# Three conversions of weights moved, and one copy: a fused attention, mixing and gating kernel on one core

## The chip, the cores and the metric

The kernel runs on one core of a Trainium2 chip. A core has five engines that run their own instruction streams: TensorE (PE) for matrix products, VectorE (DVE), ScalarE (ACT) and GpSimd (POOL) for element-wise work, and SyncE (SP), which here issues the DMAs. They wait for one another through semaphores. The metric is the time of one execution on the device, in microseconds; the lower the better.

## The reference, cut to what matters

Three blocks follow one another. `B=4`, `S=576`, 8 heads of 64 columns, so 512 model columns.

```
scores = q @ k.T / 8, masked to a window of 32 (heads 0-3) or a dilated one of 128, step 4 (heads 4-7)
x  = softmax(scores) @ v                                  # (4, 576, 512) over all heads
theta = x @ w_theta                                       # 512 x 512
y  = w_tok_r @ (x * cos(theta)) + w_tok_i @ (x * sin(theta))   # mixes the 576 tokens
u  = x + y ;  x2 = u + relu(u @ w_ch)
h  = relu(x2 @ w_in) ;  hu, hv = halves of h's 1024 columns
v_s = w_spatial @ layernorm(hv) + b_spatial               # mixes the 576 tokens
out = (hu * v_s) @ w_out
```

Everything is float32. The kernel writes a float32 factor as a rounded high part and the remainder, and makes a float32 product of three products: high by high, high by low, low by high.

## The kernel before, in words

The inputs lie with 128 rows on the partitions. In the first phase a batch goes through four steps, named after their generators. `attention(b)` makes scores (`s`), exponentials and their sums (`sm`, L343 to L350), transposed probabilities (`pt`) and values. `th_run(b)` works on tiles `t` of 128 tokens (64 in the last). It splits x into `xh` and `xl` on DVE (L435, L436; on ACT for batch 0), multiplies by `w_theta` (`ps_th`, L441), takes the sine and cosine on ACT (`ta`, `tb`, L455 to L459), multiplies by x on DVE (L462) and splits each product into `zh` and `zl`, the cosine's in tiles 0 to 3 and the sine's in 4 to 7. `tm_run(b)` mixes the tokens (`ps_y`, L512, L519) and adds to x on DVE (L522), and that sum is split again (`uh`, `ul`). `ch_run(b)` is the channel product (`ps_r`, L540) with its eviction on DVE (L543); for batch 0 its result goes to DRAM in two parts as well, `x2p`, through two buffers named `parts`. In the second phase, `hv` and its normalisation, `hu`, the spatial product `ps_sp` and the output product `ps_o` are made batch by batch.

A weight arrives as 64-bit words in two pieces, is put together by a scaling on ACT and a shift and an or on DVE (L140 to L142), rounded to a high part, and the remainder is a subtraction on POOL. `w_in` is converted once and kept in DRAM: the value half by eight units (`j_in`, to `win_d`), the u half by two times eight (`gate_half(0)`, `gate_half(1)`, to `wiu_d`): four reads and four additions or subtractions of pieces, of which seven are written. Such a write goes through a buffer with room for both parts (`kept`), and the buffer is free when its DMA has landed. The results of `j_in` and `gate_half(0)` use the two buffers `parts`; those of `gate_half(1)` use three in the attention's pool.

What is put between what is written out by hand. `spread(main, (fill, rate))` takes one step of `main` and then `rate` steps of each fill, `late` lets a load run ahead of its conversion, and `behind` keeps a unit from being moved ahead of an instruction. Within these limits a scheduler that plans with its own costs sets the order on each engine; every engine then runs its stream in that order. The stages are

```
for b in (0, 1):
    ch = ch_run(b)
    spread(chain(tm_run(b, K_ALL), take(ch, CH_BEFORE)), (attention(b + 1), ATT_RATE), (second if b else jobs(j_tok1 + j_ch), SECOND_RATE if b else TOK_RATE))
    run(th_run(b + 1, (4, 0, 1, 2, 3) if b + 1 < PAIR else (0, 1, 2, 3)))
    run(ch)
```

then `tm_run(2)` with `attention(3)`, `third`, the theta product of the last 64 tokens of batches 2 and 3 together, `th_run(3)`, `ch_run(2)` and `tm_run(3)`.

Here `second` is `j_in + gate_half(0)` at a rate of 1.5, and `third` is `gate_half(1)`. The halves of `w_spatial` and `b_spatial` (sums and differences, high and low parts: `wsp_hh`, `wsp_lb`) are computed by `w_half` (L725) in the stage of `ch_run(3)`, together with the loads of `w_in`'s u half and the normalisation of `hv`.

Of the kernel before, what the change touches and what calls it, by code (L numbers as in the profile page):

```python
# [11 lines left out]
F32 = mybir.dt.float32  # L12
# [47 lines left out]
THETA_ENG = "gg"  # L60
Z_HI = ("v", "g")

# [5 lines left out]
def tile_block(ctx: ExitStack, tc: tile.TileContext, qT, kT, vw, eye_in, mask_in, eye_b_in, w_theta, w_tok, w_ch, w_in, w_sp, w_sph, b_sp, w_out, out):  # L68
# [21 lines left out]
    x2d = [dram.tile([P, 4, S], F32, name=f"x2d{b}") for b in range(B)]  # L90
    wo_d = dram.tile([P, 4, 2, DM], F32R, name="wo_d")
    x2p = dram.tile([P, 4, 2, S], F32R, name="x2p")
    win_d = dram.tile([P, 4, 2, DM], F32R, name="win_d")
# [72 lines left out]
    def piece(src):  # L166

        st = stg.tile([P, 2 * CH], U32, tag="w64", name="w64", bufs=4)
        SY.dma_start(st[:, :DM], src.bitcast(U32))
        return st  # L170

    def kept(src, dst, t, eng="a"):

        copy(t[:, 0], src, eng)
        G.tensor_tensor(t[:, 1], src, f32(t[:, 0]), op=ALU.subtract)  # L175
        SY.dma_start(f32(dst), f32(t))

    def stored(src, dst):

        def finish(st):  # L180
            t = p1.tile([P, 2, CH], F32R, tag="parts", name="parts", bufs=2)[:, :, :DM // 2]
            kept(bits64(None, DM // 2, IN_ENG[2], st), dst, t, IN_ENG[0])

        return lambda: piece(src), finish

    def gate_half(kk):

        g = {}
        n = DM // 2
        room = []  # L190

        def out(blk, src):
            if kk == 0:
                room.append(p1.tile([P, 2, CH], F32R, tag="parts", name="parts", bufs=2)[:, :, :n])
            elif not room:
                room.append(patt.tile([P, S + WIN], F32R, tag="k", name="wiuk", bufs=2)[:, :2 * n].rearrange("p (i n) -> p i n", i=2))
                two = patt.tile([P, NT, P], F32R, tag="v", name="wiuv", bufs=2).rearrange("p t k -> p (t k)")[:, :4 * n].rearrange("p (j i n) -> p j i n", j=2, i=2)
                room.extend((two[:, 0], two[:, 1]))
            kept(src, wiu_d[:, :, blk, kk], room.pop())

# [7 lines left out]
        def add(blk, x, y, z, op):  # L208
            def finish(_):
# [210 lines left out]
    def th_unit(b, t, pair=False):  # L420
# [39 lines left out]
        if t < 4:  # L460
            for k, tt in ((t, tb), (4 + t, ta)):
                iv = V.tensor_tensor(tt, xn, tt, op=ALU.mult)  # L462
                zh[b, k], zl[b, k] = ztile(k)
                zlast[b] = ia, iv, split(zh[b, k], zl[b, k], tt, "ag"[k // 4], "g")
        else:
# [136 lines left out]

    second = late(j_in + gate_half(0), LAG_W, last_softmax)
    third = late(gate_half(1), LAG_W, last_softmax)

# [21 lines left out]
    for b in range(PAIR):  # L627
        ch = ch_run(b)
        spread(chain(tm_run(b, K_ALL), take(ch, CH_BEFORE)), (attention(b + 1), ATT_RATE), (second if b else jobs(j_tok1 + j_ch), SECOND_RATE if b else TOK_RATE))
        run(th_run(b + 1, (4, 0, 1, 2, 3) if b + 1 < PAIR else (0, 1, 2, 3)))  # L630
        run(ch)

# [5 lines left out]
    for i in range(HELD):  # L638
        with tc.issue_after(values[12 * (PAIR + 2) - HELD + i].ins):
            next(tm)  # L640
    run(third)
    run(th_shared(PAIR))
# [81 lines left out]

    def w_half():  # L725
        st, bt = stage(), stage()
        sd, bd = (stg.tile([P, CH], F32, tag="stage", name="stage", bufs=4) for _ in range(2))
        SY.dma_start(st, w_sph)
        for r in (64, 96):
            SY.dma_start(bt[r:r + 1], b_sp)  # L730
        yield
        V.tensor_tensor(sd, st[:, :CH], st[:, CH:], op=ALU.subtract)
        for r in (64, 96):
            V.tensor_tensor(bd[r:r + 1], bt[r:r + 1, :CH], bt[r:r + 1, CH:], op=ALU.subtract)  # L734
        G.memset(f32(wsp_lb[HALF:]), 0.0)
        for s_, b_, c in ((st, bt, slice(0, 2)), (sd, bd, slice(2, 3))):
            w = CH * (c.stop - c.start)
            hh, lb = (t[:, c].rearrange("p c n -> p (c n)") for t in (wsp_hh, wsp_lb))
            A.copy(hh, s_)
            V.tensor_tensor(lb[:HALF], s_[:HALF], f32(hh[:HALF]), op=ALU.subtract)  # L740
            A.copy(lb[64:65], b_[64:65])
            bh = stage()[:, :w]
            A.copy(bh[96:97].bitcast(F32R), b_[96:97])
            V.tensor_tensor(lb[96:97], b_[96:97], bh[96:97], op=ALU.subtract)  # L744
        yield

    def w_gate(kk):
# [48 lines left out]
    wsp_hh = p2s.tile([P, 3, CH], F32R, name="wsp_hh")  # L796
    wsp_lb = p2s.tile([P, 3, CH], F32R, name="wsp_lb")
    wo_h = p2s.tile([P, 4, DM], F32R, name="wo_h")
    wo_l = p2s.tile([P, 4, DM], F32R, name="wo_l")
# [51 lines left out]

    spread(ch_run(3), (chain(jobs([lambda: win_u_load(slice(0, 4)), lambda: win_u_load(slice(4, 7))]), w_half()), 0.5), (jobs([lambda t=t: hv_norm(0, t) for t in (0, 2, 1, 3)]), HV_RATE))
    wo_load()
# [303 lines left out]
```

## Time and profile before

| what | value |
|---|---|
| median of 3 runs (lowest, highest) | 536.91 us (536.36, 539.77) |
| the profiled execution, its own time | 539.95 us |
| its span | 538.2 us |
| PE, DVE, ACT, POOL busy | 96%, 66%, 56%, 40% |
| mean granted clock of PE | 0.987 of full speed |

The profiled execution lasted 1.75 us longer than its span, which is what lies around the first and last instruction. In a timeline row the first number is the start from the span's beginning, the second the time from that start to the end of the instruction or of the few that are grouped (`x3`); matmuls are pipelined and overlap. What stands in brackets at the end is how long the engine had been idle before it, and whose end is taken to have released it. A line number is one of the kernel before.

### The profile page before, as it was taken

To read this page: it belongs to the slowest core of one execution; us is meant where nothing else is said; L and a number is where in the kernel's file an instruction comes from. 1 tells how busy PE (TensorE), PEld (TensorE's weight loads), DVE (VectorE), ACT (ScalarE), POOL (GpSimd) and SP (SyncE) were. 2 spreads that over 40 slices of the span, in tenths; PEclk is the share of its full clock that TensorE was granted. 3 is DMA by queue.
4 is the path that set the end of the run, shared out by engine and by line. 5 is a ranking of instruction groups with operands and counts; after the bars stand their busy time and mean duration, and the time that the engine had idled before them with its cause. 6 is when DMAs were issued, how large, how long until landed. Compare 5 with 4: busy or idle time off the path is not lost. (4 is left out here: it accounts for less than half of the span.)

```text
span 538.2 us, 10595 instructions
## 1 busy us (share of the span) xinstructions
PE 514.8 (96%) x3764; PEld 471.2 (88%) x3764; DVE 354.7 (66%) x888; ACT 301.3 (56%) x838; POOL 215.3 (40%) x272
## 2 busy tenths in 40 slices
PE   5979989999999989999999999989999999999997
PEld 5856879988999969999889999889899789988996
DVE  2777779546656765657563588698982929799350
ACT  4878976537866537766472253355454435555332
POOL 3874875533864427515186235202401400040040
PEclk9979989999999999999999999989999999999999
DMA  8949266750557962325005949542022030201003
GB/s 229 312 166 281 73 177 201 237 177 12 159 139 217 275 219 81 100 80 181 22 1 191 367 144 363 185 159 88 2 79 88 1 117 2 89 1 60 21 1 99
DMA packets 63193, 72.55 MB, mean 135 GB/s; under 512 B 25410, under 2 KB 46402, under 8 KB 62884
## 3 DMA queue, kind: packets, MB, share of 16 engines
q1 hardware_dynamic: 60916, 71.32, 42.0%
q10 hardware_dynamic: 2224, 0.55, 0.5%
q8 instruction: 30, 0.49, 0.4%
q14 instruction: 23, 0.19, 0.1%
HBM read 52.20 MB, written 19.66 MB: 134 GB/s over the span
## 5 line engine op out<-in xcount | busy, mean ns | idle before, releaser
L413 POOL TENSOR_TENSOR gl<-hu,gh 128x288 fp32r<-128x288 f32 (+1 forms) x32 | 30.8, 975 | 144.4 <-ACT gh L117 121.8
L519 PE MATMUL ps_y<-wtok_h,zh 128*128 128x288 f32 x270 | 82.1, 306 | 1.6 <-DVE sm L343 1.6
L519 PE MATMUL ps_y<-wtok_h,zl 128*128 128x288 f32 x270 | 80.7, 300 | 0.0
L519 PE MATMUL ps_y<-wtok_l,zh 128*128 128x288 f32 x270 | 80.3, 298 | 0.0
L519 PEld LDWEIGHTS ps_y<-wtok_h,zh 128*128 128x128 f32 x270 | 51.2, 190 | 2.7 <-DVE sm L343 1.9
L519 PEld LDWEIGHTS ps_y<-wtok_h,zl 128*128 128x128 f32 x270 | 51.3, 191 | 0.3
L519 PEld LDWEIGHTS ps_y<-wtok_l,zh 128*128 128x128 f32 x270 | 51.2, 190 | 0.1
L350 POOL TENSOR_TENSOR sm<-sm,l 128x288 f32<-128x288 f32 x48 | 32.0, 669 | 40.5 <-DVE l L349 25.6
L347 ACT ACTIVATE sm<-sm,m 128x96 f32<-128x96 f32 x108 | 39.2, 365 | 6.3 <-DVE m L344 6.0
L540 PE MATMUL ps_r<-uh,wch_h 128*128 128x288 f32 x128 | 38.0, 297 | 0.3 <-DVE x L543 0.3
L540 PE MATMUL ps_r<-ul,wch_h 128*128 128x288 f32 x128 | 37.4, 296 | 0.0
L540 PE MATMUL ps_r<-uh,wch_l 128*128 128x288 f32 x128 | 37.4, 294 | 0.0
L413 POOL TENSOR_TENSOR ul<-x,uh 128x288 fp32r<-128x288 f32 x32 | 26.6, 838 | 24.7 <-ACT uh L117 24.5
L331 PE MATMUL s<-kt,qz 128*128 128x96 f32 x252 | 36.3, 284 | 0.0
L175 POOL TENSOR_TENSOR parts<-w64g,parts 128x256 fp32r<-128x256 f32 x23 | 18.0, 784 | 43.2 <-DVE parts L119 27.6
L331 PEld LDWEIGHTS s<-kt,qz 128*128 128x128 f32 x252 | 34.0, 203 | 0.7
L923 PE MATMUL ps_sp<-wsp_h,vh 128*128 128x288 f32 x112 | 32.6, 297 | 0.3 <-ACT vh L117 0.3
L923 PE MATMUL ps_sp<-wsp_h,vl 128*128 128x288 f32 x112 | 32.9, 295 | 0.0
L441 PE MATMUL ps_th<-wth_h,xl 128*128 128x512 f32 (+1 forms) x76 | 30.2, 397 | 2.6 <-DVE xl L436 2.6
L923 PE MATMUL ps_sp<-wsp_l,vh 128*128 128x288 f32 x112 | 32.6, 294 | 0.0
L441 PE MATMUL ps_th<-wth_h,xh 128*128 128x512 f32 (+1 forms) x76 | 31.0, 410 | 0.7 <-DVE xh L435 0.7
L441 PE MATMUL ps_th<-wth_l,xh 128*128 128x512 f32 (+1 forms) x76 | 29.8, 392 | 0.0
(232 smaller groups left out, 1598.8 us busy)
## 6 DMA issues: line engine op xcount, KB each, us to landing
vt<-vw SPq DMA_DIRECT2D x15, 576.0 KB, 5.5
w<-w_tok SPq DMA_DIRECT2D x18, 288.0 KB, 4.5
x2d<-x SPq DMA_DIRECT2D x32, 144.0 KB, 2.8
kt<-kT SPq DMA_DIRECT2D x15, 304.0 KB, 4.2
w<-w_in SPq DMA_DIRECT2D x16, 256.0 KB, 3.8
out<-o SPq DMA_DIRECT2D x15, 256.0 KB, 2.0
qz<-qT SPq DMA_DIRECT2D x26, 144.0 KB, 4.3
x2tl<-x2d SPq DMA_DIRECT2D x6, 576.0 KB, 4.5
```

The costliest lines, as they stand in the source:

```text
L175: G.tensor_tensor(t[:, 1], src, f32(t[:, 0]), op=ALU.subtract)
L331: PE.matmul(s[:, KW * blk:KW * (blk + 1)], qz[:, t].rearrange("p j q -> p (j q)"), kt[:, T * t:T * t + KW], start=not on_pe, stop=not on_pe)
L347: ia = A.activation(sm[:, t, :], src[:, t, :], AF.Exp, bias=m_[:, t:t + 1], scale=scale, accum_out=ls[:, t, 0:1])
L350: ig = G.tensor_tensor(sm, sm, l.unsqueeze(2).to_broadcast([P, 3, KW]), op=ALU.mult)
L413: return (G if el == "g" else V).tensor_tensor(dst_l, src, f32(dst_h), op=ALU.subtract)
L441: PE.matmul(ps, lh[:, k, :], rh[:, k, :], start=(i == 0), stop=(i == 11))
L519: PE.matmul(ps[:, :CH], lh[b, k][:, P * d:P * (d + 1)], rh[:, k, cs], start=(n == 0), stop=(n == 3 * len(ks) - 1))
L540: PE.matmul(ps[:, :CH], lh[:, k, P * e:P * (e + 1)], rh[:, k, cs], start=(n == 0), stop=(n == 11))
L923: PE.matmul(ps[:, :CH], a[i][kk], b[j][kk], start=start, stop=(kk, j) == (1, 1), skip_group_check=True)
```

## The change

1. The high parts of batch 0's cosine products (`zh`, tiles 0 to 3) are copied on DVE instead of ACT (`Z_HI`); for the other batches they stay on ACT.
2. The value half's eight conversions (`values_in`) move from the stage of batch 1's token mixing to that of `th_run(1)` and the rest of `ch_run(0)`, one per step. They may start when the first token mixing has made its last addition (`mixed[7:8]`).
3. The b=1 stage now has both halves of `gate_half`, sixteen units with fourteen results, through four buffers in turn: two new ones named `wiuz` and the two `parts` (`spot`).
4. `w_half` stands where `third` stood, uses the attention's buffers and writes the two results to DRAM (`wh_d`); `w_half_load` loads them where `w_half` had been.

```
-Z_HI = ("v", "g")
+Z_HI = ("vg", "ag")
...
+    wh_d = dram.tile([P, 2, 3 * CH], F32R, name="wh_d")
...
     def stored(src, dst):
         def finish(st):
-            t = p1.tile([P, 2, CH], F32R, tag="parts", name="parts", bufs=2)[:, :, :DM // 2]
+            t = spot() if spots else p1.tile([P, 2, CH], F32R, tag="parts", name="parts", bufs=2)[:, :, :DM // 2]
...
+    spots = []
+
+    def spot():
+        if not spots:
+            spots.extend(pz.tile([P, DM], F32R, tag=t, name="wiuz", bufs=2).rearrange("p (i n) -> p i n", i=2) for t in ("zh8", "zl8"))
+            spots.extend(p1.tile([P, 2, CH], F32R, tag="parts", name="parts", bufs=2)[:, :, :H2] for _ in range(2))
+        spots.append(spots.pop(0))
+        return spots[-1]
...
         def out(blk, src):
-            if kk == 0:
-                room.append(p1.tile([P, 2, CH], F32R, tag="parts", name="parts", bufs=2)[:, :, :n])
-            elif not room:
...
-            kept(src, wiu_d[:, :, blk, kk], room.pop())
+            kept(src, wiu_d[:, :, blk, kk], spot())
...
+    def w_half():
+        (st, bt), (hh, lb) = ([patt.tile(sh, d, tag=t, name="wsph", bufs=2) for _ in range(2)] for sh, d, t in (([P, S + WIN], F32, "k"), ([P, NT, P], F32R, "v")))
...
+            V.tensor_tensor(sd, st[:, :CH], st[:, CH:S], op=ALU.subtract)
+            G.memset(f32(lb[HALF:]), 0.0)
...
+            for i, t in enumerate((hh, lb)):
+                SY.dma_start(f32(wh_d[:, i]), f32(t))
...
-                zlast[b] = ia, iv, split(zh[b, k], zl[b, k], tt, "ag"[k // 4], "g")
+                zlast[b] = ia, iv, split(zh[b, k], zl[b, k], tt, Z_HI[b > 0][k // 4], "g")
...
-    second = late(j_in + gate_half(0), LAG_W, last_softmax)
-    third = late(gate_half(1), LAG_W, last_softmax)
+    values_in = late(j_in, 1, lambda: mixed[7:8])
+    second = late(gate_half(0) + gate_half(1), LAG_W, last_softmax)
...
-        run(th_run(b + 1, (4, 0, 1, 2, 3) if b + 1 < PAIR else (0, 1, 2, 3)))
-        run(ch)
+        spread(chain(th_run(b + 1, (4, 0, 1, 2, 3) if b + 1 < PAIR else (0, 1, 2, 3)), ch), *([] if b else [(values_in, 1.0)]))
...
-    run(third)
+    spots.clear()
+    run(late([w_half()], LAG_W, last_softmax))
...
+    def w_half_load():
+        for i, t in enumerate((wsp_hh, wsp_lb)):
+            SY.dma_start(f32(t.rearrange("p c n -> p (c n)")), f32(wh_d[:, i]))
...
-    spread(ch_run(3), (chain(jobs([lambda: win_u_load(slice(0, 4)), lambda: win_u_load(slice(4, 7))]), w_half()), 0.5), (jobs([lambda t=t: hv_norm(0, t) for t in (0, 2, 1, 3)]), HV_RATE))
+    spread(ch_run(3), (chain(jobs([lambda: win_u_load(slice(0, 4)), lambda: win_u_load(slice(4, 7)), w_half_load])), 0.5), (jobs([lambda t=t: hv_norm(0, t) for t in (0, 2, 1, 3)]), HV_RATE))
```

The scheduler's order moves with this. A row below is one instruction, or several alike in a row, with its line in its own kernel; a number behind a name tells tiles apart.

On ACT in `th_run(0)`, before, around the third cosine copy (`zh_784`; `sums_68` is a first block's exponentials, `w64g` a weight's scaling):

```order
L459 ACTIVATE tb<-tb,half_pi 128x512
L455 ACTIVATE tb<-ta 128x512
L347 ACT_TABLE_LOAD
L347 ACTIVATE sm,sums_68<-sm,m 128x96 x3
L458 ACT_TABLE_LOAD
L458 ACTIVATE ta<-ta 128x512
L459 ACTIVATE tb<-tb,half_pi 128x512
L140 ACTIVATE w64g<-w_954 128x288
L140 ACTIVATE w64g<-w_962 128x288
L140 ACTIVATE w64g<-w_1021 128x288
L117 CAST zh_784<-tb 128x512
L140 ACTIVATE w64g<-w_1029 128x288
```

and now:

```order
L488 ACTIVATE ta<-ta 128x512
L489 ACTIVATE tb<-tb,half_pi 128x512
L485 ACTIVATE tb<-ta 128x512
L488 ACTIVATE ta<-ta 128x512
L489 ACTIVATE tb<-tb,half_pi 128x512
L141 ACTIVATE w64g<-w_955 128x288
L141 ACTIVATE w64g<-w_963 128x288
L141 ACTIVATE w64g<-w_1022 128x288
L141 ACTIVATE w64g<-w_1030 128x288
L377 ACT_TABLE_LOAD
L377 ACTIVATE sm,sums_68<-sm,m 128x96 x3
L377 ACTIVATE sm,sums_69<-sm,m 128x96 x3
```

The copy is gone from ACT, and the exponentials, which stood between the sines with a table load ahead and behind, all come after the last sine. On DVE, now, the third copy (`zh_785`) stands between two pairs of products:

```order
L373 SCALAR_TENSOR_TENSOR sm<-s,masks 128x288
L492 TENSOR_TENSOR tb<-ps_xn,tb 128x512
L492 TENSOR_TENSOR ta<-ps_xn,ta 128x512
L374 TENSOR_REDUCE m<-sm 128x3
L373 SCALAR_TENSOR_TENSOR sm<-s,masks 128x288
L120 CAST zh_785<-tb 128x512
L492 TENSOR_TENSOR tb<-ps_xn,tb 128x512
L492 TENSOR_TENSOR ta<-ps_xn,ta 128x512
```

Before, DVE had no such copy. The second piece is on DVE in `th_run(1)`, with the last two `xh` of x's full tiles. Before:

```order
L450 SCALAR_TENSOR_TENSOR ta<-ta,ps_th 64x512
L435 TENSOR_SCALAR xh<-x_923 128x512
L436 SCALAR_TENSOR_TENSOR xl<-x_923,xh 128x512
L469 TENSOR_TENSOR zz<-ps_xn,tb 64x512
L470 TENSOR_TENSOR zz<-ps_xn,ta 64x512
L435 TENSOR_SCALAR xh<-x_923 128x512
L450 SCALAR_TENSOR_TENSOR ta<-ta,ps_th 128x512
L436 SCALAR_TENSOR_TENSOR xl<-x_923,xh 128x512
```

and now, `parts` being the high parts of the value half and `w64g`, `c` its pieces:

```order
L480 SCALAR_TENSOR_TENSOR ta<-ta,ps_th 64x512
L120 CAST parts<-w64g 128x256 x2
L465 TENSOR_SCALAR xh<-x_924 128x512
L466 SCALAR_TENSOR_TENSOR xl<-x_924,xh 128x512
L499 TENSOR_TENSOR zz<-ps_xn,tb 64x512
L500 TENSOR_TENSOR zz<-ps_xn,ta 64x512
L143 SCALAR_TENSOR_TENSOR w64g<-w64g,c_107 128x256
L120 CAST parts<-w64g 128x256 x2
L142 TENSOR_SCALAR c_107<-w_1943 128x256
L465 TENSOR_SCALAR xh<-x_924 128x512
L143 SCALAR_TENSOR_TENSOR w64g<-w64g,c_107 128x256
L480 SCALAR_TENSOR_TENSOR ta<-ta,ps_th 128x512
```

Two pairs of casts, and the ors and shifts of the conversion, now stand among the steps of the theta product, ahead of its last `xh`. The third is on DVE at the start of `th_run(2)`, where the last pieces of the u half are added up. Before:

```order
L142 SCALAR_TENSOR_TENSOR w64g<-w64g,c_106 128x256
L436 SCALAR_TENSOR_TENSOR xl<-x_1996,xh 128x512 x2
L543 SCALAR_TENSOR_TENSOR x_923<-ps_r,x_923 128x288 x4
L210 TENSOR_TENSOR w64g<-w64g 128x256 x3
L435 TENSOR_SCALAR xh<-x_1996 128x512
L210 TENSOR_TENSOR w64g<-w64g 128x256
L450 SCALAR_TENSOR_TENSOR ta<-ta,ps_th 128x512
L436 SCALAR_TENSOR_TENSOR xl<-x_1996,xh 128x512
```

and now:

```order
L466 SCALAR_TENSOR_TENSOR xl<-x_2077,xh 128x512
L213 TENSOR_TENSOR w64g<-w64g 128x256
L573 SCALAR_TENSOR_TENSOR x_924<-ps_r,x_924 128x288
L466 SCALAR_TENSOR_TENSOR xl<-x_2077,xh 128x512
L213 TENSOR_TENSOR w64g<-w64g 128x256
L573 SCALAR_TENSOR_TENSOR x_924<-ps_r,x_924 128x288
L213 TENSOR_TENSOR w64g<-w64g 128x256
L573 SCALAR_TENSOR_TENSOR x_924<-ps_r,x_924 128x288
L213 TENSOR_TENSOR w64g<-w64g 128x256
L573 SCALAR_TENSOR_TENSOR x_924<-ps_r,x_924 128x288
L465 TENSOR_SCALAR xh<-x_2077 128x512
L466 SCALAR_TENSOR_TENSOR xl<-x_2077,xh 128x512
```

Three of these additions stood in a row ahead of an `xh`; now four of them stand one by one between the evictions of the channel product (`ps_r`), the first of them ahead of an `xl`.

## Rows read from the trace of the kernel before

**Rows 1.** The page, part 1: busy us, share of the span, instructions per engine.

```profile
PE 514.8 (96%) x3764; PEld 471.2 (88%) x3764; DVE 354.7 (66%) x888; ACT 301.3 (56%) x838; POOL 215.3 (40%) x272
```

**Rows 2.** Windows: from:to, length, busy us by engine, PE clock, DMA share, GB/s.

```profile
73.20:76.70 3.50, 3.48 (x15) 3.49 (x16) 3.50 (x13) 2.64 (x10) 3.10 (x7) 0.52 0.94 275
100.00:150.00 50.00, 50.00 (x377) 46.23 (x376) 25.30 (x60) 31.50 (x82) 26.03 (x31) 1.00 0.39 125
240.00:260.00 20.00, 19.88 (x185) 17.73 (x185) 12.44 (x32) 11.43 (x42) 8.16 (x10) 1.00 0.43 139
353.10:356.60 3.50, 3.50 (x16) 3.50 (x16) 3.50 (x7) 2.19 (x5) 0.00 (x0) 0.52 1.03 389
```

**Rows 3.** Timeline, PE: start us, us, instruction, [idle before <- what ended it].

```profile
66.17 0.54 PE L512 MATMUL ps_y<-wtok_h,zh 128*128 128x288 f32 x2 [1.18 <-ACT zh L117]
...
67.77 0.29 PE L512 MATMUL ps_y<-wtok_l,zh 128*128 128x288 f32 x1
67.90 0.29 PE L512 MATMUL ps_y<-wtok_h,zl 128*128 128x288 f32 x1
...
73.22 0.61 PE L519 MATMUL ps_y<-wtok_h,zh 128*128 128x288 f32 x1 [1.61 <-DVE sm L343]
```

**Rows 4.** Timeline, ACT, same stretch.

```profile
65.50 0.61 ACT L117 CAST zh<-tb 128x512 fp32r<-128x512 f32 x1
...
66.49 1.28 ACT L347 ACT_TABLE_LOAD   x1
```

**Rows 5.** Timeline, DVE, same stretch.

```profile
64.57 0.69 DVE L462 TENSOR_TENSOR tb<-ps_xn,tb 128x512 f32<-128x512 f32 x1 [1.25 <-ACT tb L459]
...
72.72 0.44 DVE L343 SCALAR_TENSOR_TENSOR sm<-s,masks 128x288 f32<-128x288 f32 x1
```

**Rows 6.** Timeline, PE, theta product of batch 2.

```profile
198.63 0.50 PE L441 MATMUL ps_th<-wth_h,xh 128*128 128x512 f32 x1 [0.73 <-DVE xh L435]
...
200.69 0.50 PE L441 MATMUL ps_th<-wth_h,xl 128*128 128x512 f32 x1 [1.56 <-DVE xl L436]
```

**Rows 7.** Timeline, DVE, around those waits.

```profile
196.36 1.34 DVE L210 TENSOR_TENSOR w64g<-w64g 128x256 f32<-128x256 f32 x3 [4.52 <-POOL parts L175]
...
197.62 0.95 DVE L435 TENSOR_SCALAR xh<-x 128x512 fp32r<-128x512 f32 x1
```

**Rows 8.** Timeline, ACT, around those waits.

```profile
195.10 0.41 ACT L117 CAST parts<-w64g 128x256 fp32r<-128x256 f32 x1 [4.63 <-DMA wiu_d<-parts]
```

**Rows 9.** Timeline, PE, start of the second phase.

```profile
351.23 0.40 PE L923 MATMUL ps_hu<-x2th,winuh 128*128 128x288 f32 x1 [1.70 <-ACT hu L947]
...
352.60 0.40 PE L923 MATMUL ps_sp<-wsp_h,vh 128*128 128x288 f32 x1 [0.31 <-ACT vh L117]
```

**Rows 10.** Timeline, DVE, ahead of those waits.

```profile
340.75 0.46 DVE L732 TENSOR_TENSOR stage<-w 128x288 f32<-128x288 f32 x1 [3.89 <-DMA w<-w_sph]
```

**Rows 11.** DMA issues: out<-in, queue, xcount, KB each, median us to landing.

```profile
w<-w_sph SPq DMA_DIRECT2D x1, 288.0 KB, 13.7
```

**Rows 12.** Timeline, DVE: an or, and two casts of one shape.

```profile
164.26 0.42 DVE L142 SCALAR_TENSOR_TENSOR w64g<-w64g,c 128x256 uint32<-128x256 uint32 x1
...
164.97 0.28 DVE L119 CAST parts<-w64g 128x256 fp32r<-128x256 f32 x1
...
166.20 0.81 DVE L119 CAST parts<-w64g 128x256 fp32r<-128x256 f32 x1
```

**Rows 13.** Timeline, DVE, theta product of batch 1: the last xh.

```profile
125.04 0.43 DVE L435 TENSOR_SCALAR xh<-x 128x512 fp32r<-128x512 f32 x1 [0.48 <-PE ps_th L441]
```

**Rows 14.** Timeline, PE: that xh's first use.

```profile
127.92 0.48 PE L441 MATMUL ps_th<-wth_h,xh 128*128 128x512 f32 x1
```

**Rows 15.** DMA issues, the value half's writes.

```profile
win_d<-parts SPq DMA_DIRECT2D x8, 256.0 KB, 4.1
```

**Rows 16.** Timeline, POOL, beside the second cast of rows 12.

```profile
166.07 0.79 POOL L413 TENSOR_TENSOR ul<-x,uh 128x288 fp32r<-128x288 f32 x1
```

**Rows 17.** Timeline, POOL, place A: a low part.

```profile
66.19 1.28 POOL L413 TENSOR_TENSOR zl<-tb,zh 128x512 fp32r<-128x512 f32 x1 [2.38 <-ACT zh L117]
```

More of the change, by code (lines that the diff above doesn't have):

```diff
@@ L189, in gate_half @@
         n = DM // 2
-        room = []
         def out(blk, src):
-            if kk == 0:
-                room.append(p1.tile([P, 2, CH], F32R, tag="parts", name="parts", bufs=2)[:, :, :n])
-            elif not room:
-                room.append(patt.tile([P, S + WIN], F32R, tag="k", name="wiuk", bufs=2)[:, :2 * n].rearrange("p (i n) -> p i n", i=2))
-                two = patt.tile([P, NT, P], F32R, tag="v", name="wiuv", bufs=2).rearrange("p t k -> p (t k)")[:, :4 * n].rearrange("p (j i n) -> p j i n", j=2, i=2)
-                room.extend((two[:, 0], two[:, 1]))
-            kept(src, wiu_d[:, :, blk, kk], room.pop())
+            kept(src, wiu_d[:, :, blk, kk], spot())
         def read(q, p, blk):
@@ L216, in gate_half, with load, finish @@
                 add(3, a22, a21, a22, ALU.add), add(5, a21, a11, a21, ALU.subtract), add(4, a11, a22, a11, ALU.subtract), add(6, a12, a12, a11, ALU.subtract)]
+    def w_half():
+        (st, bt), (hh, lb) = ([patt.tile(sh, d, tag=t, name="wsph", bufs=2) for _ in range(2)] for sh, d, t in (([P, S + WIN], F32, "k"), ([P, NT, P], F32R, "v")))
+        hh, lb = (t.rearrange("p t k -> p (t k)")[:, :3 * CH] for t in (hh, lb))
+        sd = stg.tile([P, CH], F32, tag="stage", name="stage", bufs=4)
+        bd = stg.tile([P, CH], F32, tag="stage", name="stage", bufs=4)
+        def load():
+            SY.dma_start(st[:, :S], w_sph)
+            for r in (64, 96):
+                SY.dma_start(bt[r:r + 1, :S], b_sp)
+        def finish(_):
+            V.tensor_tensor(sd, st[:, :CH], st[:, CH:S], op=ALU.subtract)
+            G.memset(f32(lb[HALF:]), 0.0)
+            for r in (64, 96):
+                V.tensor_tensor(bd[r:r + 1], bt[r:r + 1, :CH], bt[r:r + 1, CH:S], op=ALU.subtract)
+            for s_, b_, c in ((st[:, :S], bt[:, :S], slice(0, S)), (sd, bd, slice(S, 3 * CH))):
+                A.copy(hh[:, c], s_)
+                V.tensor_tensor(lb[:HALF, c], s_[:HALF], f32(hh[:HALF, c]), op=ALU.subtract)
+                for r in (64, 96):
+                    A.copy(lb[r:r + 1, c], b_[r:r + 1])
+                V.tensor_tensor(lb[96:97, c], b_[96:97], f32(lb[96:97, c]), op=ALU.subtract)
+            for i, t in enumerate((hh, lb)):
+                SY.dma_start(f32(wh_d[:, i]), f32(t))
+        return load, finish
     wth = {}
@@ L723, in stage @@
         return stg.tile([P, 2 * CH], U32, tag=tag, name=tag, bufs=4).bitcast(F32)
[L725 to L745, printed above, removed]
     def w_gate(kk):
```

## The prediction

> **What bounds the kernel now.** I read the busy shares first. TensorE (PE) is busy for 514.8 of 538.2 us, the next engine for 66% [rows 1]. So the time moves only where PE stands idle, 23.4 us in all, or where it runs at its lower clock. The windows come next: PE is busy for 50.00 of 50 us between 100 and 150 us and for 19.88 of 20 between 240 and 260 us, so nothing can be gained in either and new work there can only cost; and in two short stretches the granted clock is about half (0.52 of 2.4 GHz, the 1.2 GHz level) although PE is busy throughout [rows 2]. Then the timeline of PE, for the waits that stand near the edits, and the timelines of the other engines, for what came late. There are three such places.
>
> Place A is the first token mixing of batch 0. PE waits 1.18 us for the high part zh of a product, made on ScalarE (ACT), and 1.61 us more for VectorE's (DVE) masking of scores [rows 3]. From 73.2 us on the clock is at half for 3.5 us [rows 2]. ACT makes that copy only at 65.50 us, after both sine calls, and reloads its exponential table right after it, for 1.28 us [rows 4]. DVE sits 1.25 us for ACT before one product, and reaches the masking that PE waits for at 72.72 us [rows 5].
>
> Place B is the start of the third theta product. PE waits 0.73 us for xh and 1.56 us for xl [rows 6], both DVE's. DVE had idled 4.52 us in front of three additions of the u half, for GpSimd's (POOL) earlier subtraction [rows 7]; and the copy ahead of it, on ACT, waited 4.63 us until a write to DRAM had landed and freed one of two buffers [rows 8].
>
> Place C is the start of the second phase. PE waits 1.70 us for ACT's hu and 0.31 us for vh [rows 9], and from 353.1 us on the clock is at half again for 3.5 us [rows 2]. DVE had idled 3.89 us for w_sph [rows 10], whose load took 13.7 us to land [rows 11]; the weight halves are computed in front of the normalisation that hu and vh come from.
>
> **The change part by part.** The sum is made against the profiled execution, 539.95 us, which is 3.0 us above the median of 536.91; the gain is then taken off the median.
>
> *The copy on VectorE (A).* Four 128x512 copies leave ACT for DVE, in batch 0 only. In the new order the third stands on DVE ahead of the product that had waited 1.25 us for ACT, so it is done by about 64.57 - 1.25 + 0.5 = 63.8 us, against 65.50 + 0.61 = 66.1 us before. ACT has no copy between its sines and its exponentials any more and loads two tables fewer, 2.56 us at the row's 1.28. Both PE waits lose what was late: 1.18 + 1.61 = 2.8 us. What a 128x512 copy costs on DVE has no row. A 128x256 one takes 0.28 us [rows 12], so 0.28 to 0.56; I take 0.5 because the length doubles, 2 us in all, beside idle times of DVE such as the 1.25 us. If that cover were gone, a copy would push back the masking of scores. The clock fell while PE had waited twice within seven us. With the waits gone I count the clock's loss back: fifteen matmuls at the full-speed spacing, 0.13 us between starts [rows 3], take 2.0 us instead of 3.5, so 1.5 us. A: 4.3 us.
>
> *Four buffers for the u half's sums (B).* The b=1 stage had 8 value conversions and 8 units of one u half, with 15 results through two buffers. It now has the 16 units of both u halves, 14 results through four. The load is as before and the room is double, so the 4.63 us on ACT and the 4.52 us on DVE behind it should mostly go. B: 0.73 + 1.56 = 2.3 us. Against it stands that four of these additions now lie between DVE's evictions of the channel mixing and ahead of the second xl. If the buffers were late all the same, the 4.5 us would stand there in full, 2.2 us more than PE waits now. So from 2.3 gained to 2.2 lost. I take 1.6 gained, near the upper end, because the room doubles.
>
> *The halves of w_sph by DRAM (C).* The subtractions and casts leave the start of the second phase, and with them the 3.89 us wait and what followed it on DVE. Two loads of finished halves remain, and their first use is a later product than hu's. C: 1.70 + 0.31 = 2.0 us and, for the clock, sixteen matmuls at 0.13 = 2.1 of 3.5 us, 1.4 us; 3.4 us. In exchange the computation goes to the 240 to 260 us stretch, where it takes the place of the second u half's conversions, so ACT and DVE carry less there than before. PE has 0.12 us of idle in it, so lateness would show: 0 to 1 us, I take 0.3. The two loads move three times the bytes of w_sph and stand behind the u half's loads; before their use lies more than the 13.7 us that the old load took: nothing.
>
> *The value half in th_run(1).* Eight conversions, with eight writes win_d on SP's queue, move into the stretch that PE fills wholly. On DVE two pairs of casts now stand in front of the last xh steps, and a shift, an or and two more casts near the last. Before, the last xh was done at 125.04 + 0.43 = 125.5 us [rows 13] and its first use was at 127.92 us [rows 14]: 2.45 us of room. Two casts at 0.28 us and two shifts or ors at 0.42 us [rows 12] eat 1.4 of it, still a cost of nothing. But the casts write into the same two buffers that the eight parts x2p of the held tokens use, and such a buffer comes free only when its write has landed, 4.1 us for win_d [rows 15]. One round is a cast, a subtraction (0.79 [rows 16]) and the landing, 0.28 + 0.79 + 4.1 = 5.2 us, 2.6 us per result with two buffers, 41 us for the 16 results in a stretch of 45 to 50. It just fits, so one wait or two will show. I take 1.5 us; the bounds are 0 and the rival's price below. The writes stand on SP's queue ahead of batch 2's keys and values, which had some room.
>
> Sum: 4.3 + 1.6 + 3.4 gained, less 0.3 and 1.5, is 7.5. I take off 0.5 for a remnant of A, where the exponentials now all follow the sines and the first transposed probabilities come later. So 7.0 us: 533.0 us for an execution like the profiled one, **529.9 us** for the median.
>
> **VectorE and GpSimd side by side.** A 128x256 cast took 0.28 us with POOL idle and 0.81 us [rows 12] where a POOL subtraction of 0.79 us had begun 0.13 us earlier [rows 16]; the cast ends 0.15 us after that subtraction. An xh took 0.95 us at place B [rows 7] and 0.43 us in th_run(1) [rows 13]. Four of POOL's 1.28 us subtractions [rows 17] lie in place A, beside the copies that come to DVE. The Trainium skill, page "SBUF — State Buffer", section "Terms", has the rule under "shared port pair": VectorE and GpSimd arbitrate for one pair of ports, locked for a full instruction, and the loser is blocked, not slowed. The rows agree for this cast. By that rule the copies would cost a whole subtraction each and not 0.5 us, and the sum would be that of the second rival.
>
> **Rivals.**
> 1. *The two parts buffers bind in th_run(1), and it comes out slower.* Six times (two pairs of casts, four single ones) DVE would wait a round of 5.2 us, less the 2.45 us of room: 2.7 us each, 16 us at worst, and 3 us for two falls of the clock at 1.5. For it: 41 of some 45 us are needed. Against: only eight of the sixteen writes are win_d, and the scheduler spread the casts. Half of it makes 529.9 + 9.5 = 539.4 us. It is slower by over 1% once 12.4 us are lost, five of the six waits; then about 543 us, 549 at worst. Chance 0.09; another 0.10 for a third to a half of it, 535 to 539 us.
> 2. *POOL blocks the copies.* Four copies held up to 1.28 us each bring the last one 5.1 us later; A then keeps little of its 4.3 us: 529.9 + 3.5 = 533.4 us. For it: the cast of 0.81 us. Against: DVE's idle times in A take some of it. Chance 0.14.
> 3. *The change doesn't do what it says*: a wait that is moved, not removed, with the half clock where it was (A's transposes behind the exponentials, or C's vh behind the same normalisation). Without A's and C's clocks, 529.9 + 2.9 = 532.8 us; without all of C, 533.3. Chance 0.10.
> 4. Forecast, 527 to 531.5 us: chance 0.57.
>
> **How the numbers follow.** About 1%, 5.4 us, is what a measurement of this kernel can tell from no change, so faster means under 531.5 us. The forecast is all there; of rivals 2 and 3 a sixth falls under it too, 0.04: faster 0.61. Within 1% lie the rest of 2 and 3 and the middle case of 1: 0.30. Slower 0.09. The range begins with everything gained and nothing new, 4.3 + 2.3 + 3.4 = 10.0, 526.9, and half a us for scatter, and reaches past rivals 2 and 3 into the middle case of the first: 526.4 to 536.4 us, leaving out about 0.15.
>
> **What would show it.** In the profile of the changed kernel: A, PE without a wait over 0.5 us between 60 and 75 us, and full clock there; two table loads fewer. B, no wait over 0.5 us of the theta product for xh or xl near 200 us, and ACT's copies not held by wiu_d writes. C, hu and vh on time at 345 to 355 us, full clock. For the first rival: PE idle between 115 and 150 us, with DVE's casts or ACT's waiting for win_d or x2p. For the second: DVE copies in A of over 1 us. The prediction is wrong if PE idles more than 3 us between 100 and 200 us, or if the half-clock stretches are found again.

## The result, and the profile after

The changed kernel takes 530.92 us in the median of 4 executions (530.21 to 532.94), the kernel before 536.63 us (535.19 to 539.77): a ratio of 0.9899, with a 95% interval from 0.9868 to 0.9930. Run again beside 23 more executions of the kernel before, it came out at 0.9899 once more (0.9865 to 0.9933). So it is 5.4 us faster, 1.0%, where 7.0 us had been forecast. The profiled execution took 530.21 us with a span of 528.4 us.

The page's busy line after:

```profile
PE 509.8 (96%) x3764; PEld 465.9 (88%) x3764; DVE 356.3 (67%) x893; ACT 296.8 (56%) x831; POOL 215.5 (41%) x272
```

PE idles 18.6 us instead of the 23.4 of [rows 1], and is busy for 5.0 us less with the same 3764 matmuls. The two half-clock stretches make 2.9 us of that by the prediction's count; what the rest is was not followed. The windows of the four stages (columns as in [rows 2]) show where. They stand at fixed times, and the changed kernel is some 12 us ahead by the last of them. First before, then after:

```profile
60.00:80.00 20.00, 16.72 (x119) 15.65 (x119) 14.44 (x46) 16.96 (x55) 14.88 (x20) 0.91 0.53 149
120.00:150.00 30.00, 30.00 (x205) 28.14 (x204) 17.71 (x39) 23.58 (x55) 18.93 (x21) 1.00 0.26 81
195.00:205.00 10.00, 7.71 (x40) 6.23 (x39) 7.12 (x12) 6.99 (x13) 4.22 (x6) 1.00 0.28 99
345.00:360.00 15.00, 12.99 (x82) 12.33 (x81) 14.00 (x39) 8.12 (x19) 2.46 (x4) 0.89 0.58 203
```

```profile
60.00:80.00 20.00, 19.05 (x176) 18.36 (x175) 19.61 (x57) 15.58 (x58) 18.25 (x25) 1.00 0.69 193
120.00:150.00 30.00, 29.05 (x207) 26.79 (x209) 22.98 (x57) 23.23 (x63) 24.80 (x28) 1.00 0.58 176
195.00:205.00 10.00, 10.00 (x61) 8.95 (x60) 5.68 (x10) 7.65 (x13) 6.24 (x6) 1.00 0.05 16
345.00:360.00 15.00, 14.14 (x106) 13.79 (x105) 12.90 (x30) 7.93 (x17) 0.00 (x0) 1.00 0.57 196
```

In the first mixing PE gains 2.3 us of busy time and the clock returns from 0.91 to 1.00; at the third theta product it loses nothing any more; at the start of the second phase 1.2 us come back, with the clock. The stage of the second theta product, which had no idle time, now has 0.95 us of it. The places in PE's timeline, which answer to [rows 3, 6, 9]:

```profile
62.72 0.40 PE L549 MATMUL ps_y<-wtok_h,zh 128*128 128x288 f32 x1 [0.95 <-DVE sm L373]
```

```profile
123.88 0.40 PE L570 MATMUL ps_r<-uh,wch_h 128*128 128x288 f32 x1 [0.42 <-DVE ta L480]
...
142.76 0.40 PE L549 MATMUL ps_y<-wtok_h,zh 128*128 128x288 f32 x1 [0.28 <-DVE sm L373]
```

```profile
357.68 0.49 PE L846 MATMUL ps_hv<-winvh,x2h 128*128 128x512 f32 x1 [0.86 <-ACT x2h L118]
```

One wait is left in place A, for the masking of scores again; there is none between 150 and 215 us; hu and vh are on time (no wait of PE between 330 and 357 us), but at 357.68 us PE waits for a part of x2. On DVE, the four copies of place A:

```profile
53.26 0.93 DVE L120 CAST zh<-spare 128x512 fp32r<-128x512 f32 x1
...
56.61 0.86 DVE L120 CAST zh<-spare 128x512 fp32r<-128x512 f32 x1
...
59.67 1.07 DVE L120 CAST zh<-tb 128x512 fp32r<-128x512 f32 x1
...
62.95 1.05 DVE L120 CAST zh<-tb 128x512 fp32r<-128x512 f32 x1
```

GpSimd's subtractions that ran when the first and the last of these four started:

```profile
52.61 1.30 POOL L443 TENSOR_TENSOR zl<-zz,zh 128x512 fp32r<-128x512 f32 x1 [0.59 <-ACT zh L118]
...
62.43 1.28 POOL L443 TENSOR_TENSOR zl<-ta,zh 128x512 fp32r<-128x512 f32 x1
```

The casts of the value half that wait longest, and the first `xh` behind them:

```profile
117.05 0.29 DVE L120 CAST parts<-w64g 128x256 fp32r<-128x256 f32 x1 [1.25 <-DMA x2p<-parts]
117.88 0.43 DVE L120 CAST parts<-w64g 128x256 fp32r<-128x256 f32 x1 [0.54 <-DMA x2p<-parts]
118.23 0.41 DVE L465 TENSOR_SCALAR xh<-x 128x512 fp32r<-128x512 f32 x1
...
135.24 0.35 DVE L120 CAST parts<-w64g 128x256 fp32r<-128x256 f32 x1 [1.25 <-DMA x2p<-parts]
...
139.51 0.71 DVE L120 CAST parts<-w64g 128x256 fp32r<-128x256 f32 x1 [0.67 <-DMA win_d<-parts]
```

The copies take 0.86 to 1.07 us; the first and the last end 0.28 and 0.29 us after the end of the subtraction (54.19 against 53.91 us, 64.00 against 63.71). The casts do wait for their buffers, 0.4 to 1.25 us at a time, and the `xh` behind the first pair starts right after them. On ACT, the one table load of place A (three before, at 59.50, 62.00 and 66.49 us), the last copy of the u half ahead of the third theta product (to hold against [rows 8]), and what is ahead of the x2 wait, with the last product that reads that buffer and the load's issue on SP's queue:

```profile
60.39 1.28 ACT L377 ACT_TABLE_LOAD   x1
```

```profile
189.19 0.41 ACT L118 CAST wiuz<-w64g 128x256 fp32r<-128x256 f32 x1 [0.65 <-DMA wiu_d<-wiuz]
```

```profile
356.47 1.15 ACT L118 CAST x2h<-x2tl 128x1152 fp32r<-128x1152 f32 x1 [2.61 <-DMA x2tl<-x2d]
```

```profile
351.88 0.30 PE L936 MATMUL ps_hu<-x2tl,winuh 128*128 128x288 f32 x1
```

```profile
352.20 1.19 SPq L716 DMA_DIRECT2D x2tl<-x2d  x2
```

The last copy of the u half waits 0.65 us for a buffer and ends before the theta product's first tile reaches ACT; the longest such wait on ACT is 1.38 us (at 180.98 us), where it was 4.63. The load of x2tl is issued as soon as that product has ended (352.18 us). In the transfers (columns as in [rows 11, 15]) the value half's writes land sooner than they did before:

```profile
win_d<-parts SPq DMA_DIRECT2D x8, 256.0 KB, 2.4
```

**The execution that the sum was made against was a long one.** Of 93 executions of the kernel before beside the experiments, 47 had a mean granted clock of 0.9915 or more and a median of 535.3 us, 30 lay between 0.9885 and 0.9915 with 537.6 us, and 16 below it with 539.3 us, and the profiled one (0.987, 539.95 us) is of the last kind. All ten executions of the changed kernel had 0.993 or more.

### The profile page after: what moved, and what is told of

Same layout as the page of the kernel before. It is cut to its first block, busy times and chain, and to the rows that moved or that the text cites. A ratio compares the mean times of both kernels' runs of the same rounds, so it can differ in the third digit from the quotient of the medians.

```text
span 528.4 us, 10596 instructions
## 1 busy us (share of the span) xinstructions
PE 509.8 (96%) x3764; PEld 465.9 (88%) x3764; DVE 356.3 (67%) x893; ACT 296.8 (56%) x831; POOL 215.5 (41%) x272
## 4 chain that ended last, share of the span: by engine, by line
PE 80%; DMA 7%; DVE 5%; ACT 4%; POOL 1%; issue 1%; ACTq 0%; DVEq 0%; POOLq 0%
PE ps_y L549 20%; PE ps_hv L846 9%; PE ps_r L570 9%; PE ps_o L1074 9%; PE ps_hu L936 8%; PE ps_sp L936 6%; PE ps_th L471 6%; PE s L361 4%; PE pt L390 3%; PE ps_x L404 2%; DMA x2tl<-x2d 2%; DMA qz_2wch_l<-qT 2%; DMA kt<-kT 1%; PE ps_x L408 1%; DMA x2p<-parts 1%
## 5 line engine op out<-in xcount | busy, mean ns | idle before, releaser
L141 ACT ACTIVATE w64g<-w 128x256 f32<-128x256 f32 (+1 forms) x50 | 21.6, 445 | 14.0 <-DMA w<-w_ch 3.4
```

Of the source, the lines that this page charges most:

```text
L141: A.activation(g, hw.bitcast(F32), AF.Prelu, scale=2.0**-112, alpha=2.0**32)
```

## The experiments

Lines of each edit are those of the kernel that it starts from. Where two ratios to the kernel before are subtracted, the difference is turned into time with 536 us. The runs were made on two chips of the same kind; the kernel before ran beside each.

**The copy on VectorE alone** (on the kernel before):

```
-Z_HI = ("v", "g")
+Z_HI = ("vg", "ag")
...
-                zlast[b] = ia, iv, split(zh[b, k], zl[b, k], tt, "ag"[k // 4], "g")
+                zlast[b] = ia, iv, split(zh[b, k], zl[b, k], tt, Z_HI[b > 0][k // 4], "g")
```

Expected: 

> The kernel before with the copy on VectorE alone (batch 0's four cosine copies). Sum's theory: the 1.18 and 1.61 us waits of the first mixing and the half-clock stretch from 73 us go, less a remnant of 0.5: 3.8 us faster, full clock between 60 and 80 us, PE busy for 19 of these 20 us or more (16.7 before). Blocking theory: POOL's subtractions hold the copies, DVE's masking is late instead, PE waits move by 1 us and the half clock stays: 0 to 1 us faster.

Measured: ratio 0.9947 (0.9915 to 0.9979), 2.8 us faster. Its windows, in the first mixing, at place B and at place C:

```profile
60.00:80.00 20.00, 19.06 (x176) 18.36 (x175) 19.61 (x58) 15.35 (x57) 18.09 (x26) 1.00 0.70 197
194.00:199.00 5.00, 3.48 (x9) 2.77 (x10) 3.91 (x7) 4.72 (x9) 1.65 (x3) 0.66 0.30 105
345.00:353.00 8.00, 6.50 (x34) 5.92 (x33) 7.60 (x22) 4.83 (x12) 0.00 (x0) 0.79 0.76 270
```

PE is busy for 19.06 us of the first, at full clock, as the sum's theory said, and that window is the changed kernel's to 0.01 us. In the other two the waits of places B and C are still there, and in this execution both are followed by the half clock, which the first profile showed at C alone.

**The copies back on ScalarE** (on the changed kernel: `"ag"[k // 4]` again). Expected: 

> The changed kernel with the four copies back on ScalarE. Theory of places that add up: the waits for zh and for the masking are back (2.8 us of stall) and in some executions the half clock with them (0 to 1.5 us): 3 us over the changed kernel, about 534 us. Rival (the copy matters little, since alone it gave 2.5 us with a half-clock stretch elsewhere): under 1.5 us over it.

Measured: 0.9961 (0.9931 to 0.9991), 3.3 us over the changed kernel's 0.9899. All three waits are back:

```profile
66.44 0.53 PE L542 MATMUL ps_y<-wtok_h,zh 128*128 128x288 f32 x2 [1.15 <-ACT zh L118]
...
67.79 0.40 PE L542 MATMUL ps_y<-wtok_h,zl 128*128 128x288 f32 x1 [0.37 <-POOL zl L443]
...
73.48 0.40 PE L549 MATMUL ps_y<-wtok_h,zh 128*128 128x288 f32 x1 [1.60 <-DVE sm L373]
```

So the copy is worth 2.8 us by itself and 3.3 us in the whole, and it is the largest part.

**The copies on GpSimd** (on the changed kernel):

```
-Z_HI = ("vg", "ag")
+Z_HI = ("gg", "ag")
```

Expected: 

> The changed kernel with batch 0's four copies on GpSimd instead of VectorE. Theory (leaving ScalarE is what counts; on VectorE each copy of some 0.45 us waits for a GpSimd subtraction and takes 0.86 to 1.07): VectorE gets 3.9 us back, GpSimd gets 2.5 us more in the same stretch, and PE's wait near 63 us stays between 0 and 1.5 us: within 1.5 us of the changed kernel. Rival (GpSimd is the late one there): waits for zl of 1 to 3 us in the first mixing, 533 us or more.

Measured: 0.9988 (0.9961 to 1.0014): the whole gain is gone. PE's timeline, and ACT's ahead of it:

```profile
64.20 0.91 PE L361 MATMUL s<-kt,qz 128*128 128x96 f32 x6 [0.81 <-DVE sm L373]
...
68.63 0.91 PE L361 MATMUL s<-kt,qz 128*128 128x96 f32 x6 [2.31 <-DVE sm L373]
```

```profile
57.12 1.28 ACT L377 ACT_TABLE_LOAD   x1
...
58.91 1.28 ACT L488 ACT_TABLE_LOAD   x1
...
61.47 1.28 ACT L377 ACT_TABLE_LOAD   x1
```

Neither theory named this. It isn't zl that is late: ACT has lost the copies, but in the order that the scheduler made for this kernel it still goes from sines to exponentials and back, with three table loads. DVE then idles 2.21 us for a cosine and is late with its masking, for which PE waits 3.1 us, and the granted clock is at half afterwards. In the fourteen profiles here, before, after and of the experiments, the eight with the copies on VectorE have one table load between 54 and 72 us, and the six others have three and the waits. So it isn't enough that the copies leave ACT: what goes with the gain each time is ACT's order, all exponentials behind the last sine. No run changes that order alone.

**The moved conversions and the four buffers alone** (the changed kernel, with `"ag"[k // 4]`, and `w_half` where it had been). Expected: 

> The changed kernel without its copy on VectorE and with w_sph's halves where they were: only the moved conversions and the four buffers are left. Sum's theory: 1.6 to 2.3 us gained at the third theta product, 0.7 to 1.5 lost in the second: 0.8 us faster, at most 1.6. Rival (the two parts buffers bind): what is gained at 200 us is lost between 115 and 150 us, 0 or slower.

Measured: 0.9983 (0.9947 to 1.0018), 0.9 us faster, within what can be told from none. The profile has the pieces: PE idles 0 us at 195 to 205 us, 0.98 us at 120 to 150 us.

**Two buffers instead of four** (on the changed kernel, in `spot`):

```
-            spots.extend(pz.tile([P, DM], F32R, tag=t, name="wiuz", bufs=2).rearrange("p (i n) -> p i n", i=2) for t in ("zh8", "zl8"))
```

Expected: 

> The changed kernel with only the two parts buffers for the u half's fourteen sums instead of four. If the buffers are what removed the waits at the third theta product: waits for xh or xl of 1.5 to 2.3 us are back near 195 us and the time is about 2 us over the changed kernel's, 533 us. If the order of the pieces did it (no value half in that stage, writes spread), nothing comes back: 531 us.

Measured: 0.9928 (0.9898 to 0.9957), 1.6 us over the changed kernel; the two intervals overlap. A wait is back, of the size expected though not for xh or xl. PE's timeline, and ACT's ahead of it:

```profile
206.60 0.40 PE L569 MATMUL ps_r<-uh,wch_h 128*128 128x288 f32 x1 [1.86 <-DVE ta L479]
```

```profile
189.63 0.41 ACT L118 CAST parts<-w64g 128x256 fp32r<-128x256 f32 x1 [2.90 <-DMA wiu_d<-parts]
...
197.54 0.41 ACT L118 CAST parts<-w64g 128x256 fp32r<-128x256 f32 x1 [1.43 <-DMA wiu_d<-parts]
```

ACT's copies wait for a buffer again, 2.90 and 1.43 us, and the sines and DVE's `ta` come later with them. So by this profile the buffers do remove the wait; which result of the theta step carries it depends on the order.

**Own buffers for the value half** (on the changed kernel; the flag `ring` is set back where `spots` is cleared):

```
-            t = spot() if spots else p1.tile([P, 2, CH], F32R, tag="parts", name="parts", bufs=2)[:, :, :DM // 2]
+            t = spot() if ring[0] else p1.tile([P, 2, CH], F32R, tag="parts", name="parts", bufs=2)[:, :, :DM // 2]
...
-    def spot():
+    def spot(more=False):
...
+        if more and len(spots) < 4:
             spots.extend(p1.tile([P, 2, CH], F32R, tag="parts", name="parts", bufs=2)[:, :, :H2] for _ in range(2))
```

Expected: 

> The changed kernel with two buffers of their own for the value half's eight conversions (the two wiuz), so that they don't share the two parts with the held tokens' eight results. Theory (the shared buffers cause the 0.42, 0.28 and 0.25 us waits between 120 and 145 us): these waits go, 0.5 to 1 us faster than the changed kernel, about 530 us. Rival (DVE's added work itself causes them): they stay, same time.

Measured: 0.9935 (0.9910 to 0.9961), 1.9 us over the changed kernel. Both theories miss. PE's timeline has the 0.42 and 0.28 us replaced by more:

```profile
131.03 0.40 PE L572 MATMUL ps_r<-uh,wch_h 128*128 128x288 f32 x1 [2.35 <-DVE x L575]
...
147.54 0.68 PE L551 MATMUL ps_y<-wtok_h,zh 128*128 128x288 f32 x3 [1.57 <-ACT zh L118]
```

With the buffers apart, the scheduler placed the casts differently, DVE's eviction x came 2.35 us late for PE, and the casts still waited up to 1.35 us for win_d, eight writes through two buffers. What the best order would give was not tried, and what causes the 0.42 and 0.28 us waits stays open.

**The halves of w_sph by DRAM alone** (on the kernel before: the new `w_half`, run after `third`, and `w_half_load`). Expected: 

> The kernel before with the halves of w_sph computed after the u half's second conversions and brought back by DRAM, nothing else changed. Sum's theory: the hu wait of 1.70 and the vh wait of 0.31 us go, and the half-clock stretch from 353 us: 3.4 us faster, less 0.3 in the stage that now has both the conversions and the halves. Rival (a wait that is moved): PE waits for something else at the same place (normalisation, x2h) and the half clock stays: within 1 us of before.

Measured: 1.0107 (1.0067 to 1.0147), 5.7 us slower, which neither theory expected. At 345 to 360 us there is no wait for hu or vh, as the theory said. But `third` is still there, and the stage then does two works:

```profile
240.00:290.00 50.00, 46.65 (x328) 41.31 (x327) 33.96 (x66) 30.64 (x68) 26.39 (x29) 1.00 0.27 92
```

PE idles 3.35 us in it, before 0.40 (49.60 of 50 busy). At 423.82 us it waits 2.40 us more for DVE's hu, at an output product for which PE waits 0.8 us at most in the other thirteen profiles. The rest of the 5.7 us isn't shown by this one profile. As far as this run goes, C and the moved conversions belong together: the halves can go to that place because the second u half has left it.

**w_sph's halves where they were** (on the changed kernel: `w_half` of the kernel before in the stage of `ch_run(3)`, no `wh_d`). It was run twice. Expected the first time: 

> The changed kernel with the halves of w_sph computed at the start of the second phase, as before. Theory: hu waits 1.7 to 2.8 us again, the half clock at about 350 us comes back in most executions: 3 us over the changed kernel, about 534 us. Rival (the load was late only by its place in the queue, and with fewer writes in front it is not): the hu wait stays under 1 us and the time is that of the changed kernel, 531 us.

Measured: 0.9909 (0.9873 to 0.9944), 0.5 us over the changed kernel, though its profile shows the full wait and the half clock after it:

```profile
346.15 0.40 PE L925 MATMUL ps_hu<-x2th,winuh 128*128 128x288 f32 x1 [2.76 <-ACT hu L949]
```

Expected the second time: 

> The kernel with w_sph's halves at the start of the second phase, again, beside the changed kernel on one chip. If the hu wait of 2.8 us and the half clock behind it are in every execution: 3 us over the changed kernel. If they are in the profiled execution more than in the others, whose clocks were 0.993 to 0.997 the first time: the profiled one is the slowest of its runs again, and the median is within 1 us of the changed kernel's.

Measured: 0.9933 (0.9908 to 0.9958), on one chip with the changed kernel's 0.9899: 1.8 us over it. Neither reading came out as written: the profiled execution is the second fastest of the twelve, and the median is more than 1 us over the changed kernel's. The profile:

```profile
343.47 0.40 PE L925 MATMUL ps_hu<-x2th,winuh 128*128 128x288 f32 x1 [0.68 <-ACT hu L949]
...
344.84 0.40 PE L925 MATMUL ps_sp<-wsp_h,vh 128*128 128x288 f32 x1 [0.31 <-ACT vh L117]
```

Kernel and place are the same; the wait is 2.76 us in one execution and 0.68 in the other, and the granted clock falls only behind the first. The load of w_sph landed after 13.2 us there and after 12.2 us here. The other profiles with `w_half` and its load in that place: 13.7 us and 1.70 [rows 9, 11], 13.0 and 2.76 (the moved conversions alone), 11.8 and 0.91 (the kernel before again), 11.5 and 1.20 (the copy alone). So the wait is 1.7 to 2.8 us with a landing of 13.0 us or more, and 0.7 to 1.2 us with 12.2 or less; within each group it doesn't follow the landing. All three with 13.0 us or more had the half clock behind the wait; of the others, the copy alone had it too.

**The same, with the load issued earlier:**

```
-    spread(ch_run(3), (chain(jobs([lambda: win_u_load(slice(0, 4)), lambda: win_u_load(slice(4, 7))]), w_half_2()), 0.5), (jobs([lambda t=t: hv_norm(0, t) for t in (0, 2, 1, 3)]), HV_RATE))
+    wh = w_half_2()
+    spread(ch_run(3), (chain(take(wh, 1), jobs([lambda: win_u_load(slice(0, 4)), lambda: win_u_load(slice(4, 7))]), wh), 0.5), (jobs([lambda t=t: hv_norm(0, t) for t in (0, 2, 1, 3)]), HV_RATE))
```

Expected: 

> The same, with w_sph's load issued ahead of two of the four loads of the u half. Theory (the load is late because it stands behind 3.5 MB of other loads): it lands some 4 us earlier, DVE's wait for it (3.5 us) and PE's for hu (2.8 us) go, and without the 0.9 us wait for x2h that the changed kernel has there, it is as fast as the changed kernel or up to 1 us faster. Rival (the work of the halves on DVE and ACT at that place is late whatever the load): the hu wait stays over 1.5 us.

Measured: 0.9894 (0.9859 to 0.9929), 530.48 us: the same as the changed kernel. The load, and the wait for hu:

```profile
w<-w_sph SPq DMA_DIRECT2D x1, 288.0 KB, 9.1
```

```profile
343.91 0.40 PE L926 MATMUL ps_hu<-x2h,winuh 128*128 128x288 f32 x1 [0.45 <-ACT hu L958]
```

The load lands 3 to 4 us sooner after its issue, and the wait is 0.45 us, with all the work of the halves still in its old place. So what was late there was the load behind the u half's loads, not the work.

**The changed kernel again** (nothing edited). Expected: 

> The changed kernel once more, beside the next two on one chip. Both theories: no half clock outside the first 40 us, mean clock 0.993 to 0.997 in nearly all runs; ratio to before 0.990.

Measured: 0.9899, clocks 0.994 to 0.996 in its six executions, and no half clock in the profile behind the first 40 us, as expected.

**The kernel before again** (nothing edited). Expected: 

> The kernel before once more, as a second profile of it and for the scatter of its runs. If the two half-clock stretches of the first profile (73 us, 353 us) belong to the kernel, they are there again, and every execution has a mean granted clock of about 0.987. If they come only in some executions, this profile has none or one of them, the mean clock of the runs spreads from 0.983 to 0.997, and the runs with 0.993 or more are 4 to 5 us faster than those under 0.988, with the waits of the three places in all of them. The ratio to before is 1.

Measured: 1.0012 (0.9981 to 1.0043), with clocks from 0.986 to 0.994. The half clock came at place A and not at place C, so the stretches come only in some executions. PE's timeline in place A:

```profile
66.25 0.53 PE L512 MATMUL ps_y<-wtok_h,zh 128*128 128x288 f32 x2 [1.18 <-ACT zh L117]
...
67.61 0.40 PE L512 MATMUL ps_y<-wtok_h,zl 128*128 128x288 f32 x1 [0.37 <-POOL zl L413]
67.85 0.33 PE L512 MATMUL ps_y<-wtok_l,zh 128*128 128x288 f32 x1
67.98 0.44 PE L512 MATMUL ps_y<-wtok_h,zl 128*128 128x288 f32 x1
68.22 0.44 PE L512 MATMUL ps_y<-wtok_l,zh 128*128 128x288 f32 x1
...
73.29 0.40 PE L519 MATMUL ps_y<-wtok_h,zh 128*128 128x288 f32 x1 [0.50 <-DVE sm L343]
```

The first two waits are those of the first profile to 0.01 us. But the half clock sets in right behind them (0.24 us between starts from 67.98 us on, 0.13 before), not behind the third; and the third is then 0.50 us instead of 1.61. PE goes on at 73.29 us here and at 73.22 us there [rows 3]. Here the half-clock stretch in front of the wait was paid out of the wait.

## Why the prediction was right

The forecast was 529.9 us, range 526.4 to 536.4; the direction, the three places and the engines behind them held. The gain was forecast too large: A, C and the clock all came out smaller than their terms, and the prices of the value half and of the computation in its new place came out smaller too, which made up a part. Step by step:

- **A, 4.3 less 0.5 us: held, a little large.** Alone 2.8 us, undone 3.3. The step that I had put last, two table loads fewer and no copy between the sines and the exponentials, goes with the gain in all fourteen profiles, and the copies on GpSimd show that to leave ACT isn't enough; that this order is the cause was not tried by itself. The waits of 3.16 us [rows 3, and 0.37 for zl between them] became 0.95 us, twice the remnant that I had set, and more than the 0.5 us that I had allowed one wait there. A copy on DVE took 0.86 to 1.07 us and not 0.5, and the masking that PE waits for stands behind three of them, on a DVE with no idle time from 52.05 us on.
- **POOL beside the copies: the second rival's mechanism, at a smaller price.** The sum had the copy alone about right: a 64x512 cast, with as many elements on each partition, takes 0.41 to 0.42 us elsewhere in this profile. But POOL ran one subtraction or copy after another beside the four, and each of them ended 0.28 or 0.29 us after the end of the subtraction that was running when it started. The same holds, within 0.27 to 0.29 us, for all 32 such copies of the eight profiles that have them. The `xh` of 0.95 us in [rows 7] also ends 0.28 us after a POOL subtraction (198.57 against 198.29 us); the one of 0.43 us in [rows 13] had POOL idle for its first 0.25 us. That is the blocking of the second rival. The Trainium skill's page "SBUF — State Buffer", section "Terms", says it would be so: the loser is blocked for as long as the other's instruction holds the ports. The trace agrees. What the rival had wrong is the price: a copy starts somewhere within a subtraction and waits only for the rest of it, so it lost 0.4 to 0.7 us over the 0.42, not up to 1.28. On PE it cost about half a microsecond over the remnant; DVE's idle time in the stretch (busy for 14.44 of 20 us before, 19.61 now) took the rest.
- **B, 1.6 us: held.** Both waits, 2.29 us, are gone, and with two buffers 1.6 us come back, in intervals that overlap.
- **The value half in th_run(1), 1.5 us lost: held in kind.** The casts wait for x2p and win_d, and PE idles 0.95 us in 120 to 150 us, 0.70 of it for DVE's `ta` and `sm` in the rows above; that the casts' waits are what made these late is not shown, since buffers of their own only brought other waits. win_d landed after 2.4 us, not the 4.1 of [rows 15], which I had carried over from the stage that it left. With 2.4 the prediction's round is 3.5 us, and sixteen results need 28 of the 45 to 50 us and not 41; the first rival stayed small.
- **C, 3.4 less 0.3 us: the term that was mis-sized.** It measured 0.5 and 1.8 us in two comparisons. The wait of 2.01 us was one draw: the load's landing varies, and with 11.5 to 12.2 us the wait for hu was 0.7 to 1.2 us in three profiles. The 0.3 us for the computation in its new place did not show: PE is busy for 50.00 us between 225 and 275 us. A term that I had not set is a new wait: PE waits 0.9 us for x2h, behind ACT, behind the load x2tl (2.61 us). It stands in both profiles of the changed kernel and in those of its four variants that bring the halves back by DRAM, and in none of the four profiles in which the conversions are moved and the halves computed in place. The two loads of finished halves are not what makes x2tl late. They were issued some 31 us before it; x2tl's load is issued in all fourteen profiles as the last `ps_hu` product that reads its buffer ends, and ACT's cast starts 4.3 to 4.5 us later in all of them, with the two loads or without. The kernel with the halves by DRAM alone has both loads and not this wait. What differs is PE's order: in the six profiles with the wait PE is ready for the next `ps_hv` 4.6 us after that issue, in the others it starts it after 5.9 us or more, and load and cast take 5.4 to 5.6. It is the third rival in small, a wait that takes the place of another.
- **The clock, 2.9 us of the sum (1.5 in A, 1.4 in C): counted in full, worth about half by an estimate.** The profile of before had both stretches, its second profile one: the 93 executions have a median of 536.7 us, and 535.3 us where the clock was 0.9915 or more, so I put the stretches at 1.4 us of the median. A mean clock doesn't tell the stretches apart, though: the profile with the copies back on ScalarE has 0.994 and still a half-clock stretch at 76 us. From 535.3 to the changed kernel's 530.4 us (the median of its ten executions) are 4.9 us for the waits; with 1.4 that is 6.3 us by medians, against 5.4 by the ratio.

Alone, the three parts give 2.8, 0.9 and, undone, 0.5 to 1.8 us: 4.2 to 5.5 us, which is the 5.4 us of the whole within their intervals. Put on the kernel before by itself, C loses 5.7 us, so that part has a worth only beside the other two changes.

## What to carry to other kernels

A profile is one execution: before its stalls and half-clock stretches are added up, hold its mean clock and time against the other runs, and count what only the long ones show by its share, not in full. Where a scheduler sets the order, a moved copy can be worth the order that it brings about more than its own duration: look on the engine that it leaves for what now stands together, here the exponentials behind the last sine; the same copies moved to another engine brought another order and no gain. When work at one place waits for a load, move the load's issue before moving the work: it gave the same time as the detour by DRAM, with an edit of two lines.

## What the runs showed of the hardware that was not expected

- The same waits are followed by the half clock in one execution and not in another. At place A it began behind the third wait in one profile of the kernel before and behind the first two in the other. In the kernel with w_sph's halves by DRAM alone, the waits of 1.2, 0.4 and 1.6 us were all there and the clock stayed at its upper level:

```profile
60.00:80.00 20.00, 16.59 (x140) 15.27 (x138) 15.75 (x48) 16.23 (x55) 14.10 (x19) 1.00 0.60 162
```

- VectorE's 128x512 copy beside GpSimd's subtractions was held until the running subtraction had ended, and itself ended 0.27 to 0.29 us after it, about half a microsecond late a time. GpSimd's own copies, 0.62 us in the profile with all of them on GpSimd, took 0.79 to 0.80 us in the same stretch.
